# First stage of a spectral-filter kernel: half a column table mirrored on VectorE, angle arithmetic on GpSimd, statistics of two tiles on VectorE, 64-row products in fours

## Chip, cores and metric

The kernel runs on one core of one Trainium2 chip. The metric is the device time of one execution in microseconds (us). Five engines work side by side, each through its own instructions in program order: TensorE (PE; its weight loads are PEld), VectorE (DVE), ScalarE (ACT), GpSimd (POOL) and SyncE (SP), whose queue issues the transfers here. [...]

## What is computed

```
def _A_ref(x, w_r, w_i):
    X = rfft2(x.astype(float32), axes=(-2, -1))
    X = X * (w_r + 1j * w_i)
    return irfft2(X, s=(S, D)).astype(bfloat16)

def _B_ref(x, w_gate, w_up, w_down):
    return (gelu(x @ w_gate) * (x @ w_up)) @ w_down

h  = x + _A_ref(layernorm(x), A_w_r, A_w_i)
h2 = h + _B_ref(layernorm(h), B_w_gate, B_w_up, B_w_down)
```

S = 2048 rows, D = 576 columns, a hidden width of 4608, all data in bfloat16. `layernorm` subtracts the mean of a row and divides by its standard deviation.

## The kernel before

Everything is written as matrix products. The 2048 rows lie as 16 tiles of 128 partitions (row = 16 * partition + tile). The Fourier transform over rows is split in two: products with a 128-row table `F16` (called F in the profile) inside each tile, then products with twiddle tables. The transform over columns is a product with a cosine and sine table `DT` of 3 x 128 rows and 2 x 145 columns, and `DF`, two quarters of its third block. The stages, in order of time:

1. **First stage** (0 to about 25 us). Tables are made: POOL writes index ramps (`iota`), angles are reduced to a range that a sine can take, ACT takes the sines. Beside that each row tile is normalised. Its statistics come either from ACT (`ln_act`, L120 to 123: two passes, one for the sum and one for the squares, then POOL's `ln_fin`, L125 to 128) or from DVE (`ln_dve`, L114 to 118: two half-row passes and one that joins them). POOL makes the factor 1/standard deviation for four tiles at a time (`ln_rstd`, L130 to 133: an addition and a power). DVE writes the normalised tile `xn` (L136). PE multiplies it by `F16` (`row16`, L288 to 306: four products with 128 columns, L298, and two with the 64 leftover columns, `row16_rest`, L308). ACT copies the results out of PSUM into `Bt` (`evict`, L322; `evict4` for the leftover columns, L328).
2. **Column products and twiddles.** For one index after another, six products of `Bt` with `DT` and `DF` (`f2`, L479), a copy out of PSUM into `pq` (`f2_out`, L490), eight products with the twiddle table `TF` (`f3`, L496 and L497), a copy into `g` and `hs` (L518), sums and differences `xab` (L529), the multiplication with the weights (`wmul`, L547 to 568, all DVE), and the products of the inverse transform (`i3`, L587).
3. The inverse over columns (L638), the sum over rows (L770), the second normalisation.
4. The feed-forward part (L898 to L960), from 68 us to the end.

The order of the work is written by hand: a manual schedule is in force, so each engine runs its instructions in the order in which the Python calls stand. Lines 355 to 451 are that order for the first stage. `norms(lo, hi)` normalises tiles and issues their row products, `sd` asks for DVE statistics, `angle_a`, `angle_b`, `angle_c` reduce the angles of the twiddle table, `sine` and `cosine` (L253, L256) fill `TF`, `col_sin` (L347) fills `DT`, `turn_tf` (L262) transposes `TF` by DMA into `TI`. The twiddle table is done in two parts: `first` (2 of 9 blocks, 256 columns) and `rest` (7 blocks, 896 columns). All of its angles are made on DVE, as whole numbers: a multiplication with addition (L236), a mask by 2047 (L246), a subtraction (L247) and the removal of the sign (L223). The angles of `DT` are made on POOL up to a multiple of D (`kd`, L198, L199) and finished on DVE (`phases`, L268, and `drop_sign`).

POOL also runs two indirect gathers of weight rows (L381), clears `DF` and the `Zt` tiles (L387, L400) and halves two weight columns (L413). SP's queue issues the input, the two copies of the gathered weights (L411), `turn_tf(first)`, 13 copies of `DT` into `DQ` (L421), `turn_tf(rest)`, and then the weights of the later stages.

PSUM is held as four slots of two banks (`two`, L66), used in turn by `f2t`, `f4`, `pt`, `pq_ps`, `gh_ps` and so on: a product that opens a slot waits until the copy of its last user is done. `fill` (L283) issues products that nobody reads, 14 before tile 0, 8 before tile 8, 5 before tile 12 and 3 before `pt`, in places where PE would be idle.

Of the kernel before, what the change touches and what calls it, by code (L numbers as in the profile page):

```python
# [29 lines left out]
NFT = F // P  # L30
NR = D // 64
NDT = 5
JW = 58
NW = JP // JW
FQ = 3
# [6 lines left out]
def kernel_body(  # L42
# [140 lines left out]
    iota(kv[:, 0:7], [[1, 7]], 1)  # L183
    iota(kv[:, 7:9], [[8, 2]])
    q16 = tmp("q16", [P, P], FP32)
    iota(q16[:], [[16, P]])
# [4 lines left out]
    iJ = tmp("iJ", [P, JP], FP32)  # L191
    iota(iJ[:], [[1, 2], [2, JH]])
    iDs = tmp("iDs", [P, 3], FP32)
    G.tensor_scalar(iDs[:], iD[:], 1.0 / D, None, op0=ALU.mult)
    pd, kd = tmp("pd", [P, 3, JP], FP32), tmp("kd", [P, 3, JP], FP32)
    C23 = 8388608.0
    for t in range(3):
        G.tensor_scalar(kd[:, t, :], iJ[:], iDs[:, t : t + 1], C23, op0=ALU.mult, op1=ALU.add)  # L198
# [13 lines left out]
    ia, s2a, s2p = tmp("ia", [P, 1]), tmp("s2a", [P, 1], FP32), tmp("s2p", [P, 1], FP32)  # L212
    V.tensor_scalar(ia[:], ip[:], 7, None, op0=ALU.bitwise_and)
    V.tensor_scalar(s2a[:], ia[:], 127.0 / 8.0, None, op0=ALU.mult)
    V.scalar_tensor_tensor(s2p[:], ip[:], 0.125, s2a[:], op0=ALU.mult, op1=ALU.add)
    ks = tmp("ks", [P, 9], FP32)
    V.tensor_scalar(ks[:], kv[:], s2p[:, 0:1], None, op0=ALU.mult)
    V.tensor_scalar(iu[:], iu[:], 7, None, op0=ALU.bitwise_and)
    mask = tmp("mask", [P, P], FP32)
    V.tensor_scalar(mask[:], iu[:].rearrange("p c l -> p (c l)"), 0.0, None, op0=ALU.is_equal)  # L220

    def drop_sign(dst, src):
        V.tensor_scalar(  # L223
# [5 lines left out]
            op1=ALU.logical_shift_right,  # L229
        )  # L230

    pr, ab = tmp("pr", [P, 9, P]), tmp("ab", [P, 9, P], FP32)

    def angle_a(sl):
        n = sl.stop - sl.start
        V.scalar_tensor_tensor(  # L236
            pr[:, sl],
            q16[:].unsqueeze(1).to_broadcast([P, n, P]),
            s2p[:, 0:1],
            ks[:, sl].unsqueeze(2).to_broadcast([P, n, P]),  # L240
            op0=ALU.mult,
            op1=ALU.add,
        )

    def angle_b(sl):
        V.tensor_scalar(pr[:, sl], pr[:, sl], 2047, None, op0=ALU.bitwise_and)  # L246
        V.tensor_scalar(ab[:, sl], pr[:, sl], -1024.0, None, op0=ALU.add)  # L247

    def angle_c(sl):
        drop_sign(ab[:, sl], ab[:, sl])  # L250

    def sine(sl):
        A.activation(TF[:, sl, 2, :], pr[:, sl], ACT.Sin, bias=pib[:], scale=-2.0 * PI / S)  # L253

    def cosine(sl):
        A.activation(TF[:, sl, 1, :], ab[:, sl], ACT.Sin, bias=nhpib[:], scale=2.0 * PI / S)  # L256

    def minus_sine(sl):
        V.tensor_scalar(TF[:, sl, 0, :], TF[:, sl, 2, :], -1.0, None, op0=ALU.mult)
# [5 lines left out]

    def phases():
        for t in range(3):
            V.scalar_tensor_tensor(  # L268
                pd[:, t, :], iJ[:], iD[:, t : t + 1], kd[:, t, :], op0=ALU.mult, op1=ALU.add
            )  # L270

    def row_table():
        V.tensor_tensor(
            F16[:, 0:2, :],
            fs[:].unsqueeze(1).to_broadcast([P, 2, P]),
            mask[:].unsqueeze(1).to_broadcast([P, 2, P]),
            ALU.mult,
        )
        V.tensor_scalar(F16[:, 2, :], F16[:, 0, :], -1.0, None, op0=ALU.mult)

    ps_f = {}

    def fill(dst, n):  # L283

# [3 lines left out]
    def row16(h):  # L288
        if h % 2 == 0 or h == H - 1:
            ps_f[h] = two("f2t")  # L290
        if h % 4 == 0:
            ps_f["f4", h] = two("f4")
        f2t, b = (ps_f[h], 0) if h in ps_f else (ps_f[h - 1], 1)
        fill(f2t[:, b, :], {0: 14, 8: 8, 12: 5}.get(h, 0))
# [10 lines left out]
        if h < 12:  # L305
            row16_rest(h)

    def row16_rest(h):  # L308
        o = (h % 4) * P
# [17 lines left out]
    def evict4(h):  # L327
# [2 lines left out]
            ps_f["f4", h][:, 0].rearrange("p (h c l) -> p h c l", h=4, c=16),  # L330
        )

    def sd(*hs):
        for h in hs:
            ln_dve(mv, h)

    def norms(lo, hi):
        for h in range(lo, hi):
# [1 line left out]
            row16(h)  # L340

    wm = [tmp(n, [P, 8 * J], BF16) for n in ("wm_r", "wm_i")]
    xn_pool = tc.tile_pool(name="xn", bufs=1, side="right")
    xn = xn_pool.__enter__().tile([P, H, D], BF16, name="xn")

    def col_sin(r, src, bias):
        A.activation(  # L347
            DT[:, :, :, r, :],
            src[:].rearrange("p t (a j) -> p t a j", a=2),
            ACT.Sin,  # L350
            bias=bias[:],
            scale=-2.0 * PI / D,
        )

    first, rest = slice(0, 2), slice(2, 9)
    ln_act(1)
    ln_act(3)
    sd(0)
    row_table()
    sd(2)  # L360
    ln_fin(slice(1, 4, 2))
    ln_rstd(rstd, mv, 0, 4)
    sd(4, 6)
    norms(0, 4)
    ln_act(5)
    ln_act(7)
    ln_fin(slice(5, 8, 2))
    ln_rstd(rstd, mv, 4, 8)
    ln_act(9)
    evict(0)  # L370
    ln_act(11)
    evict4(0)
    evict(2)
    angle_a(first)
    angle_b(first)
    angle_c(first)
    sine(first)
    cosine(first)
    norms(4, 8)
    for t, w in zip(wm, (A_w_r, A_w_i)):  # L380
        G.indirect_dma_start(  # L381
            out=t[:],
            out_offset=None,
            in_=w.rearrange("(a r) j -> a (r j)", r=8),
            in_offset=bass.IndirectOffsetOnAxis(ap=rev[:, 0:1], axis=0),
        )
    G.memset(DF[:], 0.0)  # L387
    ln_fin(slice(9, 12, 2))
    sd(8, 10)
    ln_rstd(rstd, mv, 8, 12)  # L390
    evict(4, 6)
    evict4(4)
    ln_act(13)
    sd(12, 14)
    norms(8, 12)
    sd(15)
    ln_fin(slice(13, 14))
    ln_rstd(rstd, mv, 12, 16)
    for z in Zts:
        G.memset(z[:].rearrange("p a w b j -> p (a w b) j")[:, :, JW:], 0.0)  # L400
    phases()
    drop_sign(kd[:], pd[:])
    evict(8, 10)
    evict4(8)
    col_sin(1, pd, zerob)
    col_sin(0, kd, hpib)
    norms(12, 16)
    minus_sine(first)

    for w, t in ((WR, wm[0]), (WI, wm[1])):  # L410
        nc.sync.dma_start(w[:, 9 : H + 1, 0:J], t[:].rearrange("p (r j) -> p r j", r=8))  # L411
    for w in (WR, WI):
        G.tensor_scalar(w[:, :, 0 : J : J - 1], w[:, :, 0 : J : J - 1], 0.5, None, op0=ALU.mult)  # L413
    turn_tf(first)
    for r in (1, 0):
        for w in range(1 - r, NW):
            j0, j1 = w * JW, (w + 1) * JW
# [7 lines left out]
    for h in range(12, 16):  # L425
        row16_rest(h)
    evict(12, 14, 15)
    angle_a(rest)
    V.tensor_copy(DF[0:32], D3[0:32])
    V.tensor_copy(DF[96:128], D3[96:128])  # L430
    evict4(12)
    angle_b(rest)
    pt = two("pt")
    fill(pt[:, 1, :], 3)
    for x in range(2):
        for p0 in (0, 64):
# [4 lines left out]
                start=True,  # L441
                stop=True,
            )
    for sign in range(2):
        A.activation(
            G16[:, sign, :, :].rearrange("p x q -> p (x q)"),
            pt[:, 0, 0 : 2 * P],
            ACT.Copy,
            scale=G_SCALE if sign == 0 else -G_SCALE,
        )  # L450
    sine(rest)

    xn_pool.__exit__(None, None, None)
    spw = tc.tile_pool(name="spw", bufs=1)
# [565 lines left out]
```

## Time and profile before

| | us |
|---|---|
| median of 3 runs | 497.54 (497.31 to 497.56) |
| the profiled execution's own time | 497.44 |
| its span, first to last instruction | 495.66 |
| PE busy in the span | 487.6 |
| DVE, ACT, POOL busy in the span | 224.9, 161.6, 29.3 |
| first row product (L298) starts | 9.12 |
| first column product (L479) starts | 25.16 |
| first copy of `g` (L518) starts | 28.20 |
| first `xab` (L529) starts | 28.89 |
| first inverse product (L587) starts | 34.28 |
| feed-forward part starts | 68.36 |

Times of single instructions are microseconds from the start of the span. The profile gives for each engine its busy time, the busy share in 40 slices, the chain of work that ended last, and, as a timeline, each instruction with its start, its duration, its line and its operands.

### The profile page before, as it was taken

Reading aid. Unit: us, or ns where it says so; the run is one execution under the profiler, and the core shown is the slowest. Engines: PE = TensorE matmul, PEld = TensorE weight load, DVE = VectorE, ACT = ScalarE, POOL = GpSimd, SP = SyncE. Lnnn points to the kernel's source line nnn. Section 1 sums busy time; section 2 is a strip of 40 time slices with the busy share of each in tenths; the row PEclk is TensorE's granted clock in tenths of the full one; section 3 lists DMA queues with packets and bytes.
Section 4 is the critical chain, followed back from the end, with each engine's and each line's share of the span. In section 5 each row is a group of like instructions: output and inputs, shape, how many; then the busy total and the mean of one; then the engine's idle time right before and its main releaser. Section 6 shows DMA issues by size and latency. Waiting matters only on the chain.

```text
span 495.7 us, 12763 instructions
## 1 busy us (share of the span) xinstructions
PE 487.6 (98%) x5714; PEld 337.6 (68%) x5716; DVE 224.9 (45%) x443; ACT 161.6 (33%) x289; POOL 29.3 (6%) x78
## 2 busy tenths in 40 slices
PE   6999999999999999999999999999999999999997
PEld 3478789885579965555599855555799655555995
DVE  8999884698632157433311244333221333333111
ACT  8999873322211022323300123223110233232000
POOL 8500010011110001000000000000000000000000
PEclk9999999999999999999999999999999999999999
DMA  8739779969990039988730079977700288870000
GB/s 291 214 52 201 207 148 207 185 107 211 213 210 4 3 84 180 209 166 153 145 73 3 1 177 187 199 153 147 144 3 1 79 156 158 156 149 2 13 15 24
DMA packets 89549, 62.33 MB, mean 126 GB/s; under 512 B 23190, under 2 KB 88086, under 8 KB 89494
## 3 DMA queue, kind: packets, MB, share of 16 engines
q1 hardware_dynamic: 89206, 60.34, 61.5%
q0 software_dynamic: 288, 1.18, 0.8%
q8 instruction: 44, 0.72, 0.7%
q14 instruction: 11, 0.09, 0.1%
HBM read 52.65 MB, written 2.36 MB: 111 GB/s over the span
## 4 chain that ended last, share of the span: by engine, by line
PE 95%; POOL 2%; DVE 1%; ACT 1%; issue 0%; POOLq 0%
PE gu L898 57%; PE acc L941 27%; PE pq_ps L479 2%; PE cs_ps L638 2%; PE acc L960 2%; PE eo_ps L587 2%; PE y_ps L770 1%; PE gh_ps L497 1%; PE gh_ps L496 1%; DVE xn L136 1%; POOL rstd L133 0%; PE f2t L298 0%; ACT DT L347 0%; ACT Bt L322 0%; POOL kd L198 0%
## 5 line engine op out<-in xcount | busy, mean ns | idle before, releaser
L898 PE MATMUL gu<-Bt,wgu 64*128 64x512 bf16 (+1 forms) x2646 | 270.6, 363 | 0.0
L898 PEld LDWEIGHTS <-wgu 64*128 64x128 bf16 x2646 | 151.8, 94 | 115.3 <-issue 0.3
L907 DVE TENSOR_TENSOR P_sb<-g_sb,gu 128x512 bf16<-128x512 f32 (+1 forms) x156 | 100.4, 645 | 140.3 <-ACT g_sb L906 140.3
L906 ACT ACTIVATE g_sb<-gu 128x512 f32<-128x512 f32 (+1 forms) x156 | 88.0, 564 | 193.5 <-PE gu L898 193.5
L941 PEld LDWEIGHTS <-P_sb 64*128 64x128 bf16 x2160 | 122.2, 94 | 10.9
L941 PE MATMUL acc<-wd,P_sb 64*128 64x288 bf16 x1440 | 90.9, 283 | 0.0
L950 DVE TENSOR_TENSOR part<-part,acc 128x576 f32<-128x576 f32 x15 | 11.3, 755 | 112.6 <-ACT part L949 112.6
L949 ACT COPY part<-acc 128x576 f32<-128x576 f32 x15 | 9.6, 640 | 122.8 <-PE acc L941 122.8
L941 PE MATMUL acc<-wd_a,P_sb 64*128 64x288 bf16 x720 | 46.8, 283 | 0.0
L898 PE MATMUL gu<-Bt,wgu_e 64*128 64x256 bf16 (+1 forms) x162 | 12.5, 305 | 0.0
L795 DVE TENSOR_SCALAR hrow<-h_sb,mv,rstd 128x1152 bf16<-128x1152 bf16 x14 | 12.2, 868 | 0.6 <-POOL rstd L833 0.6
L479 PE MATMUL pq_ps<-DT,Bt 128*128 128x290 bf16 x64 | 12.3, 286 | 0.0
L286 PE MATMUL f2t<-h_sb,ident 128*128 128x512 bf16 x26 | 8.3, 473 | 3.9 <-DMA h_sb<-in_A_x_dram 3.9
L133 POOL TENSOR_TENSOR rstd<-rstd,mhalf 128x1 f32<-128x1 f32 (+1 forms) x16 | 11.7, 729 | 1.3
L952 DVE TENSOR_TENSOR h_sb<-h_sb,part 128x576 bf16<-128x576 bf16 x15 | 11.4, 758 | 0.5
L898 PEld LDWEIGHTS <-wgu_e 64*128 64x128 bf16 x162 | 10.4, 94 | 1.1
L479 PEld LDWEIGHTS <-Bt 128*128 128x128 bf16 x96 | 9.2, 97 | 2.5
L132 POOL TENSOR_SCALAR rstd<-mv 128x1 f32<-128x1 f32 (+1 forms) x16 | 4.0, 247 | 116.4 <-DVE mv L118 116.1
L638 PE MATMUL cs_ps<-DQ,EO 58*128 58x290 bf16 x144 | 10.8, 283 | 0.0
L490 ACT CAST pq<-pq_ps 128x580 bf16<-128x580 f32 x15 | 9.9, 663 | 0.2
L298 PE MATMUL f2t<-F,xn 128*128 128x256 bf16 x64 | 9.3, 275 | 0.6 <-DVE xn L136 0.6
L123 ACT ACTIVATE junk<-h_sb 128x576 bf16<-128x576 bf16 x14 | 9.4, 674 | 0.6 <-DMA h_sb<-in_A_x_dram 0.6
(138 smaller groups left out, 280.0 us busy)
## 6 DMA issues: line engine op xcount, KB each, us to landing
wgu<-in_B_w_gate_dram SPq DMA_DIRECT2D x46, 432.0 KB
wgu<-in_B_w_up_dram SPq DMA_DIRECT2D x46, 432.0 KB
wd_a<-in_B_w_down_dram SPq DMA_DIRECT2D x1, 1728.0 KB
wd<-in_B_w_down_dram SPq DMA_DIRECT2D x1, 1728.0 KB
wd<-in_B_w_down_dram SPq DMA_DIRECT2D x6, 288.0 KB
out_dram<-h_sb SPq DMA_DIRECT2D x3, 576.0 KB
h_sb<-in_A_x_dram SPq DMA_DIRECT2D x4, 288.0 KB
h_sb<-in_A_x_dram SPq DMA_DIRECT2D x2, 576.0 KB
```

The costliest lines, as they stand in the source:

```text
L133: G.tensor_tensor(dst[:, sl], dst[:, sl], mhalf[:, sl], ALU.pow)
L479: T.matmul(ps[:, par, 0:JP], lhsT=Bt[:, t, col], rhs=DT[:, t // 2, par] if t < 4 else DF[:, par], start=(t == par), stop=(t == 4),)
L587: T.matmul(pv[:, n], lhsT=z[:, a, w].rearrange("p b j -> p (b j)"), rhs=TI[:, ts[k], 1 - a : 3 - a, :], start=(a == 0), stop=(a == 1),)
L638: T.matmul(ps[:, e, 0:JP], lhsT=EO[x][rows, w, 2 * g : 2 * g + 2].rearrange("p h e k l -> p (h e k l)"), rhs=DQ[rows, w] if w or e else DT ...
L795: V.tensor_scalar(hrow[:], h_sb[:, h, :].rearrange("p (r k) -> p r k", k=64).unsqueeze(2).to_broadcast([P, NR, 2, 64]), mv2[:, h, 0:1], rs ...
L898: T.matmul(gu[:, c, 0:n], lhsT=w[rows, r, i * P : (i + 1) * P], rhs=hl[tcnk % 2][rows, r, lo:hi], start=(r == 0), stop=(r == NR - 1),)
L906: A.activation(g_sb, gu[:, 0, 0:n], ACT.Gelu_apprx_tanh)
L907: V.tensor_tensor(p_sb(f)[:, lo:hi], g_sb, gu[:, 1, 0:n], ALU.mult)
L941: T.matmul(accs[i][:, c, 0:DH], lhsT=p_sb(f)[rows, st * P : (st + 1) * P], rhs=wd[f // NWA][rows, f % NWA, c * DH : (c + 1) * DH], start=( ...
L950: V.tensor_tensor(part, part, accs[1][:, :, 0:DH], ALU.add)
L952: V.tensor_tensor(hv, hv, part, ALU.add)
L960: T.matmul(acc[:, 0, 0:DH], lhsT=p_sb(f)[:, st * P : (st + 1) * P], rhs=wd[f // NWA][:, f % NWA, cc], start=(f == 0), stop=(f == NFT - 1),)
```

## The change

Seven things change, all in the first stage and at its seam with the second.

- **Column table.** `DT` has 145 columns per half; a sine is now taken for 73 of them only (`JM = 73`), and DVE writes the other 72 by copying them in reverse with a sign per partition (`mirror`, four instructions). The ramps and angles for it shrink from 290 to 146 columns.
- **Angles on POOL.** `phases` and a new `wrap` (a sum of two 438-column tensors) move from DVE to POOL. All angles of the twiddle table become fp32 arithmetic on POOL: `angle_a` adds two tensors, `angle_b` scales and rounds (two instructions with constants) and adds two tensors. DVE keeps the removal of the sign, now taken from the signed angle. The sine of `rest` moves from before the first column products to after them.
- **Statistics.** Tiles 7 and 13 move from ACT to DVE. `sd` now issues the joining instruction of a tile between the two half-row passes of the next.
- **Leftover products.** The 64-column products of four tiles are issued together after the fourth (`rests`), in one slot opened there.
- **Order.** All statistics of tiles 8 to 15 stand ahead of the normalisation of tile 8; the first part of the angles stands on POOL ahead of the factor for tiles 12 to 15; the rest of the angles stands on POOL behind it, ahead of the clearing of `Zt` and the halving of the weight columns. The mirror, the minus of the first sine and the two copies into `DF` stand on DVE directly behind the normalisation of tiles 12 to 15.
- **Fills.** 13 before tile 0 and 10 before tile 8 in place of 14, 8 and 5.
- **Small ones.** The row table is masked and written in one instruction; the negative half of `G16` is made by DVE from the positive half.

```diff
-    V.tensor_scalar(ks[:], kv[:], s2p[:, 0:1], None, op0=ALU.mult)
+    V.tensor_scalar(ks[:], kv[:], s2p[:, 0:1], 0.125, op0=ALU.mult, op1=ALU.mult)
...
     def angle_a(sl):
         n = sl.stop - sl.start
-        V.scalar_tensor_tensor(
+        G.tensor_tensor(
             pr[:, sl],
             q16[:].unsqueeze(1).to_broadcast([P, n, P]),
-            s2p[:, 0:1],
             ks[:, sl].unsqueeze(2).to_broadcast([P, n, P]),
-            op0=ALU.mult,
-            op1=ALU.add,
+            ALU.add,
         )
     def angle_b(sl):
-        V.tensor_scalar(pr[:, sl], pr[:, sl], 2047, None, op0=ALU.bitwise_and)
-        V.tensor_scalar(ab[:, sl], pr[:, sl], -1024.0, None, op0=ALU.add)
+        G.tensor_scalar(ab[:, sl], pr[:, sl], 1.0 / S, C23, op0=ALU.mult, op1=ALU.add)
+        G.tensor_scalar(ab[:, sl], ab[:, sl], -C23, -float(S), op0=ALU.add, op1=ALU.mult)
+        G.tensor_tensor(pr[:, sl], pr[:, sl], ab[:, sl], ALU.add)
     def angle_c(sl):
-        drop_sign(ab[:, sl], ab[:, sl])
+        drop_sign(ab[:, sl], pr[:, sl])
...
     def phases():
         for t in range(3):
-            V.scalar_tensor_tensor(
-                pd[:, t, :], iJ[:], iD[:, t : t + 1], kd[:, t, :], op0=ALU.mult, op1=ALU.add
-            )
+            G.tensor_scalar(pd[:, t, :], iJ[:], iD[:, t : t + 1], None, op0=ALU.mult)
+    def wrap():
+        G.tensor_tensor(pd[:], pd[:], kd[:], ALU.add)
...
+    def rests(h):
+        ps_f["f4", h] = two("f4")
+        for i in range(4):
+            row16_rest(h + i)
...
     def sd(*hs):
         for h in hs:
-            ln_dve(mv, h)
+            st = roll.tile([P, 2, 6], FP32, name="st", tag="st", bufs=3)
+            V.bn_stats(st[:, 0, :], h_sb[:, h, 0:DH])
+            flush()
+            V.bn_stats(st[:, 1, :], h_sb[:, h, DH:D])
+            agg.append((h, st))
...
     def col_sin(r, src, bias):
         A.activation(
-            DT[:, :, :, r, :],
+            DT[:, :, :, r, 0:JM],
...
+    def mirror(r):
+        for a in range(2):
+            V.tensor_scalar(
+                DT[:, :, a, r, JM - a : JH - a], DT[:, :, a, r, JM - 2 :: -1], sgn[:, r : r + 1], None, op0=ALU.mult
+            )
```

`flush` joins the statistics that are still open. The order after the change, from the statistics on:

```
    for h in (1, 3, 5, 9, 11):
        ln_act(h)
    phases()
    row_table()
    sd(0, 2)
    minus_row()
    sd(4)
    ln_fin(slice(1, 4, 2))
    ln_rstd(rstd, mv, 0, 4)
    sd(6, 7)
    flush()
    norms(0, 4)
    rests(0)
    ln_fin(slice(5, 6))
    ln_rstd(rstd, mv, 4, 8)
    wrap()
    gather(0)
    gather(1)
    evict(0, 2)
    evict4(0)
    norms(4, 8)
    rests(4)
    sd(8)
    drop_sign(kd[:], pd[:])
    sd(10, 12)
    ln_fin(slice(9, 12, 2))
    ln_rstd(rstd, mv, 8, 12)
    evict(4)
    col_sin(1, pd, zerob)
    col_sin(0, kd, hpib)
    sd(13, 14, 15)
    flush()
    G.tensor_scalar(q16[:], q16[:], s2p[:, 0:1], None, op0=ALU.mult)
    angle_a(first)
    angle_b(first)
    ln_rstd(rstd, mv, 12, 16)
    G.memset(DF[:], 0.0)
    G.memset(DT[:, :, 1, :, JH - 1], 0.0)
    norms(8, 12)
    rests(8)
    angle_c(first)
    evict(6)
    evict4(4)
    sine(first)
    cosine(first)
    norms(12, 16)
    rests(12)
    evict(8, 10)
    evict4(8)
    mirror(1)
    mirror(0)
    minus_sine(first)
    V.tensor_copy(DF[0:32], D3[0:32])
    V.tensor_copy(DF[96:128], D3[96:128])
    angle_a(rest)
    angle_b(rest)
    evict(12, 14, 15)
    evict4(12)
```

Behind it follow, as before, the clearing of `Zt`, the copies of the gathered weights, `turn_tf(first)`, the halving of the weight columns and the 13 copies into `DQ`. After the first two `f2` of the second stage:

```diff
         if i == 0:
             f2(order[0] + 8)
-            angle_c(rest)
-            cosine(rest)
             for r in range(2):
                 f2_out(order[0] + 8, V.tensor_copy, slice(r, r + 1))
+            angle_c(rest)
+            sine(rest)
+            cosine(rest)
             minus_sine(rest)
+            V.tensor_scalar(G16v[1], G16v[0], -1.0, None, op0=ALU.mult)
```

More of the change, by code (lines that the diff above doesn't have):

```diff
@@ L32 @@
 NDT = 5
+JM = 73
 JW = 58
@@ L185, in kernel_body @@
     q16 = tmp("q16", [P, P], FP32)
-    iota(q16[:], [[16, P]])
+    iota(q16[:], [[2, P]])
     make_identity(nc, ident[:])
@@ L211, in kernel_body @@
     )
[L212 to L215, printed above, removed]
+    V.tensor_scalar(iu[:], iu[:], 7, None, op0=ALU.bitwise_and)
+    odd, sgn = tmp("odd", [P, 1]), tmp("sgn", [P, 2], FP32)
+    s2p = tmp("s2p", [P, 1], FP32)
+    V.tensor_scalar(odd[:], ip[:], 1, None, op0=ALU.bitwise_and)
+    V.scalar_tensor_tensor(s2p[:], iu[:, 0, 0:1], 127.0, ip[:], op0=ALU.mult, op1=ALU.add)
+    for r, s in ((0, -2.0), (1, 2.0)):
+        V.tensor_scalar(sgn[:, r : r + 1], odd[:], s, -0.5 * s, op0=ALU.mult, op1=ALU.add)
     ks = tmp("ks", [P, 9], FP32)
[L217 to L220 removed]
+    V.tensor_scalar(ks[:], kv[:], s2p[:, 0:1], 0.125, op0=ALU.mult, op1=ALU.mult)
     def drop_sign(dst, src):
@@ L331, in evict4, with flush @@
         )
+    agg = []
+    def flush():
+        while agg:
+            h, st = agg.pop()
+            V.bn_aggr(mv[:, h, :], st[:])
     def sd(*hs):
         for h in hs:
-            ln_dve(mv, h)
+            st = roll.tile([P, 2, 6], FP32, name="st", tag="st", bufs=3)
[3 more added lines that the diff above has]
+            agg.append((h, st))
     def norms(lo, hi):
@@ L342, in kernel_body, with gather @@
     wm = [tmp(n, [P, 8 * J], BF16) for n in ("wm_r", "wm_i")]
+    def gather(i):
+        G.indirect_dma_start(
+            out=wm[i][:],
+            out_offset=None,
+            in_=(A_w_r, A_w_i)[i].rearrange("(a r) j -> a (r j)", r=8),
+            in_offset=bass.IndirectOffsetOnAxis(ap=rev[:, 0:1], axis=0),
+        )
     xn_pool = tc.tile_pool(name="xn", bufs=1, side="right")
@@ L364, in kernel_body @@
+    flush()
     norms(0, 4)
-    ln_act(5)
-    ln_act(7)
-    ln_fin(slice(5, 8, 2))
+    rests(0)
+    ln_fin(slice(5, 6))
     ln_rstd(rstd, mv, 4, 8)
-    ln_act(9)
-    evict(0)
-    ln_act(11)
+    wrap()
+    gather(0)
+    gather(1)
+    evict(0, 2)
     evict4(0)
-    evict(2)
+    norms(4, 8)
+    rests(4)
+    sd(8)
+    drop_sign(kd[:], pd[:])
+    sd(10, 12)
+    ln_fin(slice(9, 12, 2))
+    ln_rstd(rstd, mv, 8, 12)
+    evict(4)
+    col_sin(1, pd, zerob)
+    col_sin(0, kd, hpib)
@@ L374, in kernel_body @@
+    sd(13, 14, 15)
+    flush()
+    G.tensor_scalar(q16[:], q16[:], s2p[:, 0:1], None, op0=ALU.mult)
     angle_a(first)
     angle_b(first)
+    ln_rstd(rstd, mv, 12, 16)
+    G.memset(DF[:], 0.0)
+    G.memset(DT[:, :, 1, :, JH - 1], 0.0)
+    norms(8, 12)
+    rests(8)
     angle_c(first)
+    evict(6)
+    evict4(4)
     sine(first)
     cosine(first)
[L379 to L398, printed above, removed]
+    norms(12, 16)
+    rests(12)
+    evict(8, 10)
+    evict4(8)
+    mirror(1)
+    mirror(0)
+    minus_sine(first)
+    V.tensor_copy(DF[0:32], D3[0:32])
+    V.tensor_copy(DF[96:128], D3[96:128])
+    angle_a(rest)
+    angle_b(rest)
+    evict(12, 14, 15)
@@ L399, in kernel_body @@
+    evict4(12)
     for z in Zts:
         G.memset(z[:].rearrange("p a w b j -> p (a w b) j")[:, :, JW:], 0.0)
[L401 to L408, printed above, removed]
     for w, t in ((WR, wm[0]), (WI, wm[1])):
         nc.sync.dma_start(w[:, 9 : H + 1, 0:J], t[:].rearrange("p (r j) -> p r j", r=8))
+    turn_tf(first)
     for w in (WR, WI):
         G.tensor_scalar(w[:, :, 0 : J : J - 1], w[:, :, 0 : J : J - 1], 0.5, None, op0=ALU.mult)
-    turn_tf(first)
@@ L423, in kernel_body @@
                     )
[L425 to L432, printed above, removed]
     pt = two("pt")
@@ L443, in kernel_body @@
             )
[L444 to L451, printed above, removed]
+    G16v = [G16[:, sign].rearrange("p x q -> p (x q)") for sign in range(2)]
+    A.activation(G16v[0], pt[:, 0, 0 : 2 * P], ACT.Copy, scale=G_SCALE)
     xn_pool.__exit__(None, None, None)
```

35 lines of the change are left out of this document (16 added, 19 removed).

## Prediction

> **What bounds the kernel now.** I read the busy shares in 40 slices first, to see which stage has idle time, then the chain of work that ended last, then the timeline of each engine from 0 to 38 us.
>
> ```profile
> PE   6999999999999999999999999999999999999997
> DVE  8999884698632157433311244333221333333111
> ACT  8999873322211022323300123223110233232000
> POOL 8500010011110001000000000000000000000000
> ```
>
> PE is full from the second slice to the end (487.6 of 495.7 us), so time can only be won or lost where the first stage hands over to PE. POOL is nearly free after 25 us, which is the room that the change uses. The chain of work across the seam:
>
> ```profile
> 19.90 1.01 ACT Bt L322
> ...
> 21.28 1.95 ACT DT L347 x2
> 23.23 0.91 ACT Bt L322
> ...
> 25.22 2.34 PE pq_ps L479 x18
> ```
>
> In the tail of the first stage ACT ends last: a copy, 1.95 us of column sines, three more copies to 25.10, and then the column products (first one at 25.16 in the timeline). From there PE has no gap until 34.03. What follows hangs on the copy of `g`, behind the twiddle sines on ACT, and on DVE:
>
> ```profile
> 25.80 1.04 ACT L253 ACTIVATE TF<-pr,pib 128x896 bf16<-128x896 int32 x1
> 26.74 0.64 ACT L490 CAST pq<-pq_ps 128x580 bf16<-128x580 f32 x1
> 27.26 1.06 ACT L256 ACTIVATE TF<-ab,nhpib 128x896 bf16<-128x896 f32 x1
> 28.20 0.65 ACT L518 CAST g<-gh_ps 128x578 bf16<-128x578 f32 x1
> ```
>
> ```profile
> 28.89 1.43 DVE L529 TENSOR_TENSOR xab<-g,gh_ps 128x578 bf16<-128x578 bf16 x2 [0.74 <-ACT g L518]
> ...
> 34.09 0.76 DVE L547 TENSOR_TENSOR m<-xab,WR 128x1156 bf16<-128x1156 bf16 x1
> ...
> 37.66 0.76 DVE L547 TENSOR_TENSOR m<-xab,WR 128x1156 bf16<-128x1156 bf16 x1
> ```
>
> `xab` starts when `g` is copied, and from 28.89 DVE runs without a gap, one index per 3.57 us (34.09 to 37.66); PE's inverse products wait about 0.2 us for it each time. So whatever moves the start of the `g` copy (28.20) moves the rest of the program by as much. That start is the yardstick of all sums below.
>
> **Without mutual holds.** ACT loses two tiles of statistics (2 x 2 passes of 0.67, L123: 2.7 us), 0.75 of column sines (438 elements in place of 870; between the 256-element sine of 0.51 and the 870-element one of 1.04 the slope is 0.86 ns, so 0.66 each) and one G copy (0.28). It is no longer last.
>
> DVE loses the angles (L236 0.48 and 1.14, L246, L247, L223, `phases` 1.33), and gains two tiles, four mirrors and a G copy. A tile cost 0.925 (13.88 to 14.80); with the join slid between other passes it is about 0.82. Normalising tile 4 can start at 11.0 instead of 11.54, as its factor no longer waits for ACT's tile 7. Then 4 x 0.34, six tiles at 0.82, half of L223 (0.31) and a last join: tile 8 at about 17.5, 0.9 later than now (16.66), since tiles 13 and 15 now stand ahead of it.
>
> POOL, in its order: factor 4 to 7 done at 10.9, `wrap`, two gathers at about 1.0 (13.9), the factor for 8 to 11, which needs tile 10 (16.0), then `q16` 0.41, the first angles and the factor for 12 to 15 (two instructions, 1.5). One input with constants costs 0.24 at 4 elements (L132) and 0.93 at 870 (L199): 0.79 ns an element. A sum of two long tensors on POOL stands nowhere in the trace: the rows are L127 and L128, 2 elements, 0.19. It can't be cheaper than one input (0.79 ns), and I take as its upper end both operands read one after the other (1.58 ns): 256, 438 and 896 elements are 0.39 to 0.59, 0.54 to 0.88, 0.90 to 1.61. I take the upper ends, since two operands are streamed. The first angles are then 2.6 us, the factor stands at 20.4 (now 20.96), and tile 12 is normalised then (now 21.00). Four tiles 1.36, four mirrors at 0.19 (L259, 0.22 for 256 bf16), minus 0.14, two `DF` copies 0.6, the leftover copy 0.7: the first column product at 24.0, 1.1 earlier.
>
> That gain is given back before the yardstick. Now the sine of `rest` runs ahead of the `pq` copy and `g` follows the first product by 3.04 us. After the change DVE has the two copies of the second product first (it ends 1.65 after the first product starts; 0.74), then the sign (0.63), then ACT the cosine (1.06): `g` follows by about 4.0. 24.0 + 4.0 = 28.0 against 28.20. This would be no change.
>
> **The hold.** Now the rows that decide. POOL and DVE hold each other when both work on SBUF:
>
> ```profile
> 4.41 1.19 POOL L198 TENSOR_SCALAR kd<-iJ,iDs 128x290 f32<-128x290 f32 x2
> ```
>
> ```profile
> 4.84 0.37 DVE L273 TENSOR_TENSOR F<-fs,mask 128x256 bf16<-128x256 f32 x1
> 5.25 0.40 DVE L279 TENSOR_SCALAR F<-F 128x128 bf16<-128x128 bf16 x1
> ```
>
> ```profile
> 23.64 0.29 DVE L429 COPY DF<-DT 32x580 bf16<-32x580 bf16 x1
> 23.94 0.43 DVE L430 COPY DF<-DT 32x580 bf16<-32x580 bf16 x1
> ```
>
> ```profile
> 23.77 0.40 POOL L413 TENSOR_SCALAR WI<-WI 128x34 bf16<-128x34 bf16 x1 [1.80 <-DVE pr L236]
> ```
>
> L279 takes 0.40 for 128 elements where L259 takes 0.22 for 256; the POOL pair beside it ends at 5.60, and L279 at 5.64. The two `DF` copies are alike, but the one that meets the halving of WI takes 0.43 instead of 0.29, and ends 0.2 behind it. POOL is held too: its 2-element L128 at 9.41 takes 0.38 instead of 0.19 while tiles are normalised, and yet it gets in between two of them. So they alternate, each waiting for the whole instruction of the other. Now the POOL instructions are short where DVE needs SBUF. After the change they are long, right there.
>
> Step by step at the upper prices: `wrap` (10.9 to 11.8) holds tile 4 by 0.6, and tile 8 is normalised at 18.3. Tiles 8 to 11 and the first angles hold each other, and the factor is ready at 21.4 (+1.0). The clearing of `DF` (0.60, L387) holds tile 12, which ends at 22.2. Then the four instructions of `rest` come one by one (1.6, 1.1, 1.1, 1.7 with their own waits of 0.1), and one DVE instruction passes between each two: tile 13 ends at 23.9, tile 14 at 25.0, tile 15 at 26.1. No row shows a copy that reads in reverse; held by nothing, the mirrors end at 26.9, and held as the copies are, behind the last POOL instruction, at 28.3. I take the first. The minus, `DF` and the leftover copy, partly held, end at 29.0. First column product 29.05, `g` at 33.1: **+4.9 us**. Held mirrors make it +6.0. With sums at 0.79 ns the whole is 2.1 to 2.3 less: +2.8.
>
> [...]
>
> **What costs nothing.** Four fills fewer and the leftover products in fours lie in PE's waits for tiles 4 and 8 (with fills or without, PE waits there). SP's order is unchanged; its 13 `DQ` copies (24.14 to 34.00) start as late as the first minus, but are read first at 50.83, and `turn_tf(rest)` lands at 39.8 for a product at 41.5, which shifts too. The halving of the weights on POOL moves behind `rest` and ends near 29; its first reader, the multiplication with the weights (L547), comes only after `xab`, past 34.
>
> **The rivals.**
> - *DVE keeps its turn.* If back-to-back DVE instructions don't let POOL in, DVE runs through from 21.4 to 24.2, and the four instructions of `rest` start then: 5.3 us to 29.5, sine and cosine 2.0, `g` at 31.5: +3.3, 500.7. Against it speaks L128 getting in at 9.41.
> - *No hold of long instructions.* All holds shown are 0.1 to 0.2 us long. If a long POOL instruction leaves DVE room, the sum without holds stands: `g` at 28.0 to 28.3, 497.4.
> - *Faster.* As before, and POOL's first angles take at most 1.2 us instead of 2.6. Then tile 12 is normalised right behind tile 11 at 19.2, the first column product comes at 22.9 and `g` at 26.9: −1.3, 496.1. It decides from where the factor for 12 to 15 is ready by 19.2; the 0.24 that even 4 elements cost on POOL speaks against it.
>
> **How the numbers follow.** The profiled execution took 497.44, its span 495.66 with 1.78 around it; the median of the runs is 497.54, 0.10 more. Forecast 497.44 + 4.9 = 502.3, chance 0.58, with its own range 500.0 to 505.0. DVE keeps its turn 0.18, no hold 0.15, faster 0.09. A measurement of this kernel can tell 0.2% (1.0 us) from no change. Slower 0.58 + 0.18 = 0.76, same 0.15, faster 0.09. The range is 497.0 to 505.0: it takes in the case without holds and both prices, and leaves out the faster one and the tail above +7.6 (0.08).
>
> **What would show it.** The first column product near 29, `g` near 33, tiles 13 to 15 taking over 0.9 each in place of 0.42 and ending just behind a POOL instruction, and the feed-forward part starting 4 to 6 us later than 68.36. [...] Tiles 13 to 15 at 0.42 beside a long POOL instruction would make the forecast wrong; a tile 12 before 19.5 would make the faster rival right.

## Result and profile after

The changed kernel takes 505.09 us (median of 6 runs, 504.98 to 506.86); the kernel before, on the same chip, 497.55 (497.31 to 498.30). The ratio is 1.016, 95% interval 1.0144 to 1.0177. The forecast was 502.3, its range ended at 505.0. The direction and the place were right, and so was the mutual hold of POOL and DVE, but the forecast left the mirrors out of it; the size was too small by 2.8 us.

The profiled execution took 505.04, its span 503.3. The busy shares in 40 slices:

```profile
PE   5679999999999999999999999999999999999997
DVE  6879976489651127633312145333212233333111
...
POOL 8840000011110001100000000000000000000000
```

PE's row is new in its first three digits only (6, 9, 9 before), and POOL is now busy through its second slice (8, before 5) and into its third (4, before 0). The whole loss lies ahead of the third slice's end. The chain of work that ended last, from the fourth group of tiles on:

```profile
21.74 1.05 POOL rstd L134
22.79 0.03 issue
22.81 4.47 DVE xn L137 x4
27.29 2.92 DVE DT L387 x4
...
30.31 0.35 DVE DF L444
...
31.02 0.70 DVE Bt L335
...
31.76 1.66 PE pq_ps L507 x12
...
34.97 1.04 ACT TF L256
36.01 0.53 ACT g L546
```

Before, ACT ended last here; now POOL and then DVE do. Four tiles take 4.47 us and four mirrors 2.92. The yardstick, the start of the first `g` copy, is 35.91 in the timeline in place of 28.20: 7.7 later, and the span is 7.6 longer. Behind it nothing is lost or won: the feed-forward part starts at 75.96 in the chain of work in place of 68.36, again 7.6 later. The next two fences are DVE's and POOL's timelines of the changed kernel (start, duration, line): tiles 13 to 15 and the first mirror, and the four instructions of the rest of the angles.

```profile
23.46 1.78 DVE L137 TENSOR_SCALAR xn<-h_sb,mv,rstd 128x576 bf16<-128x576 bf16 x1
25.16 1.10 DVE L137 TENSOR_SCALAR xn<-h_sb,mv,rstd 128x576 bf16<-128x576 bf16 x1
26.18 1.10 DVE L137 TENSOR_SCALAR xn<-h_sb,mv,rstd 128x576 bf16<-128x576 bf16 x1
27.21 2.54 DVE L387 TENSOR_SCALAR DT<-DT,sgn 128x216 bf16<-128x216 bf16 x1
```

```profile
23.32 1.76 POOL L237 TENSOR_TENSOR pr<-q,ks 128x896 f32<-128x896 f32 x1
25.16 0.94 POOL L245 TENSOR_SCALAR ab<-pr 128x896 f32<-128x896 f32 x1
26.18 0.94 POOL L246 TENSOR_SCALAR ab<-ab 128x896 f32<-128x896 f32 x1
27.21 2.08 POOL L247 TENSOR_TENSOR pr<-pr,ab 128x896 f32<-128x896 f32 x1
```

Read them as pairs. Each DVE instruction ends 0.16 to 0.17 behind its POOL partner (23.46 + 1.78 = 25.24 against 25.08), the mirror 0.46 behind (short POOL clears follow there). A tile that takes 0.42 alone took as long as whatever POOL did beside it: 1.78, 1.10 and 1.10 beside 1.76, 0.94 and 0.94. That is the alternation of the forecast.

### The profile page after: what moved, and what is told of

Its sections match the earlier page's. It is cut to its first block, busy times and chain, and to the rows that moved or that the text cites. A ratio compares the mean times of both kernels' runs of the same rounds, so it can differ in the third digit from the quotient of the medians.

```text
span 503.3 us, 12756 instructions
## 1 busy us (share of the span) xinstructions
PE 487.6 (97%) x5712; PEld 339.1 (67%) x5712; DVE 227.8 (45%) x445; ACT 158.7 (32%) x280; POOL 39.0 (8%) x90
## 4 chain that ended last, share of the span: by engine, by line
PE 92%; POOL 3%; DVE 3%; ACT 1%; issue 0%; POOLq 0%
PE gu L928 56%; PE acc L971 26%; PE cs_ps L666 2%; PE pq_ps L507 2%; PE acc L990 2%; PE eo_ps L615 2%; DVE xn L137 1%; PE y_ps L800 1%; POOL rstd L134 1%; PE gh_ps L525 1%; PE gh_ps L524 1%; DVE DT L387 1%; POOL pd L268 0%; PE eo_ps L639 0%; PE pt L869 0%
## 5 line engine op out<-in xcount | busy, mean ns | idle before, releaser
L971 PEld LDWEIGHTS <-P_sb 64*128 64x128 bf16 x2160 | 122.2, 94 | 10.9
L302 PEld LDWEIGHTS <-xn 128*128 128x128 bf16 x64 | 6.1, 106 | 10.4 <-DVE xn L137 9.1
L137 DVE TENSOR_SCALAR xn<-h_sb,mv,rstd 128x576 bf16<-128x576 bf16 x16 | 10.3, 703 | 3.4 <-POOL rstd L134 3.4
L292 PE MATMUL f2t<-h_sb,ident 128*128 128x512 bf16 x23 | 6.8, 456 | 3.7 <-DMA h_sb<-in_A_x_dram 3.7
```

The costliest lines, as they stand in the source:

```text
L137: eng.tensor_scalar(dst, h_sb[:, h, :], m[:, h, 0:1], r[:, h : h + 1], op0=ALU.subtract, op1=ALU.mult)
L302: T.matmul(f2t[:, b, t * 2 * P : (t + 1) * 2 * P], lhsT=x[:, d0 : d0 + P], rhs=F16[:, n : n + 2, :], start=(n == 0), stop=(n == 1),)
L971: T.matmul(accs[i][:, c, 0:DH], lhsT=p_sb(f)[rows, st * P : (st + 1) * P], rhs=wd[f // NWA][rows, f % NWA, c * DH : (c + 1) * DH], start=( ...
```

## Experiments

**Is it POOL, and what about it?** Five kernels are the kernel before with sums on POOL that nothing reads, behind the factor for tiles 12 to 15.

```diff
     ln_rstd(rstd, mv, 12, 16)
+    for i in range(3):
+        G.tensor_tensor(
+            dm[0:128],
+            dm[0:128] if i else q16[0:128].unsqueeze(1).to_broadcast([128, 7, P]),
+            ks[0:128, 2:9].unsqueeze(2).to_broadcast([128, 7, P]),
+            ALU.add,
+        )
```

*Three long sums.* Expected:

> The kernel before, with three sums of 128x896 fp32 added on POOL behind the factor for tiles 12 to 15; nothing reads their result, each reads the one before it. Hold theory (a DVE instruction with one source in SBUF waits for the whole POOL instruction, and one passes between two): POOL runs them from 21.0 to 26.9 (1.76 to 2.08 each), tiles 12, 13 and 14 end just behind one each (22.9, 24.9, 27.0), tile 15 takes 0.42; minus, angles of rest, two DF copies and the leftover copy follow, first column product 30.1 in place of 25.16, time +5.0, 502.5. Rival (POOL off the path costs nothing to DVE, and the slow tiles of the changed kernel have another cause): tiles at 0.42, 497.5.

Measured 503.23 (502.97 to 503.68), ratio 1.0112 (1.0095 to 1.0129): +5.7. The second sum in POOL's timeline and tile 13 in DVE's:

```profile
22.77 1.68 POOL L401 TENSOR_TENSOR dm<-dm,ks 128x896 f32<-128x896 f32 x1
```

```profile
22.78 1.84 DVE L136 TENSOR_SCALAR xn<-h_sb,mv,rstd 128x576 bf16<-128x576 bf16 x1
```

The tiles end at 22.86, 24.62, 26.78 and 27.11 where 22.9, 24.9, 27.0 and 27.4 were expected. POOL work that nobody waits for cost DVE its own length here: tiles of 1.79 and 1.84 beside sums of 1.68, where a tile alone takes 0.42. The leftover copy ends at 30.03 as forecast, but the first column product starts at 30.97: PE, which had waited for the tiles, had a granted clock (the share of its full clock, as the profile shows it) of 0.50 to 0.54 from 26 to 32, so some 0.9 us of the profiled execution's loss is the clock's, estimated from the 30.1 expected for that start.

*The same sums on 32 partitions.*

```diff
-            dm[0:128],
+            dm[0:32],
```

The inputs are cut in the same way. Expected:

> The same three sums on 32 of the 128 partitions: the same number of elements for each partition, a quarter of the bytes. Hold of whole instructions: as with 128 partitions, tiles 12 to 14 end at 22.9, 24.9 and 27.0, time +5.0, 502.5. Rival (the engines share the bytes that SBUF can move): a quarter of the tiles' extra time at most, time +0.5 to +1.2, 498.0 to 498.7.

Measured 503.04 (502.53 to 503.24), +5.5; sums of 1.67, tiles of 1.79 and 1.83. A quarter of the bytes changed nothing (+5.7 with all of them), so it is not a sharing of all the bytes that move. A sharing inside each partition would look the same here; the next experiment leaves the work of each partition as it was.

*The same sums in short pieces.*

```diff
+    for i in range(3):
+        for k in range(7):
+            G.tensor_tensor(
+                dm[:, k], dm[:, k] if i else q16[:], ks[:, 2 + k : 3 + k].to_broadcast([P, P]), ALU.add
+            )
```

Expected:

> The same sums of 128 partitions cut into 21 instructions of 128 elements each, as much work in all. Hold of whole instructions: a DVE instruction waits for one piece of about 0.3 at most, tiles 12 to 15 take about 0.7 each, tile 15 ends at 23.9, and the minus, the angles and the DF copies wait about 0.25 each: time +1.5 to +2.5, 499.0 to 500.0. Rival (shared bytes): the same work, so the same as the three long sums, +5.0. If POOL's pieces come without a gap for DVE, worse than that: +6 or more.

Measured 498.93 (498.92 to 499.01), +1.4. Tile 13 in DVE's timeline:

```profile
21.49 0.50 DVE L136 TENSOR_SCALAR xn<-h_sb,mv,rstd 128x576 bf16<-128x576 bf16 x1
```

The same work in 21 pieces costs a quarter, and not all of that is holds: `g` starts 1.0 late (29.16), and later the multiplication with the weights waits 0.71 for POOL's halving, which stands behind the pieces. Tiles and pieces still alternate one to one, a pair every 0.42 to 0.43, though a tile alone takes 0.34 from start to start and a piece 0.39: by these lengths only a part of each instruction kept the other out. So the cost went with the length of the single POOL instruction (+5.7 with three sums of 1.68), and a sharing inside the partitions falls too.

*Tiles in the form with two sources.*

```diff
+                V.scalar_tensor_tensor(
+                    xn[:, h, :],
+                    h_sb[:, h, :],
+                    mv[:, h, 0:1],
+                    rstd[:, h : h + 1].to_broadcast([P, D]),
+                    op0=ALU.subtract,
+                    op1=ALU.mult,
+                )
```

This form is used for tiles 12 to 15, beside the three long sums. Expected:

> The three long sums again, and tiles 12 to 15 normalised by the form of DVE instruction with two tensor sources (the factor, repeated along the row, is the second). If only DVE instructions with one source in SBUF are held: these tiles take 0.65 to 0.7 each beside the sums and tile 15 ends at 23.6; the minus (one source) waits until 24.9, the DF copies until 26.9, first column product 28.2, time +3.1, 500.6. If every DVE instruction that uses SBUF is held: tiles 12 to 14 end behind one sum each, and four tiles cost 0.25 more each, time +6, 503.5.

Measured 504.28 (504.15 to 504.48), +6.7: held too.

```profile
21.06 2.24 DVE L342 SCALAR_TENSOR_TENSOR xn<-h_sb,mv,rstd 128x576 bf16<-128x576 bf16 x1 [0.28 <-POOL rstd L133]
...
27.54 0.80 DVE L342 SCALAR_TENSOR_TENSOR xn<-h_sb,mv,rstd 128x576 bf16<-128x576 bf16 x1
```

These are tiles 12 and 15. Tile 15, beside short POOL work, takes 0.80; tile 12 ends 0.61 behind the sum that ends at 22.69. Here POOL waits as well: its second and third sums take 2.08 in place of 1.68.

*Two sums that needn't wait for each other.*

```diff
+    for d in range(2):
+        G.tensor_tensor(
+            dms[d][:],
+            q16[:].unsqueeze(1).to_broadcast([P, 7, P]),
+            ks[:, 2:9].unsqueeze(2).to_broadcast([P, 7, P]),
+            ALU.add,
+        )
```

Expected:

> The kernel before, with two sums of 128x896 fp32 added on POOL behind the factor for tiles 12 to 15, into different tiles, so that the second needn't wait for the first (in the three long sums each waited about 0.08 for the one before it). If DVE gets one instruction between two POOL instructions in any case: tile 12 ends 0.17 behind the first sum (22.9), tile 13 behind the second, time +2.8 to +3.2, 500.5. If DVE gets its turn only where POOL's next instruction has to wait: tile 12 stays held through both sums and the three short clears behind them, to about 24.9, tiles 13 to 15 follow at 0.34 each, time about +3.4, 501.0; the end of tile 12 tells the two apart.

Measured 500.95 (499.96 to 502.51), +3.5. The times spread too far to tell the two apart (the profiled execution is the one of 499.96, the only one with a granted clock of 1.00 over its whole span), but the trace does: tile 12 ends at 22.53, 0.17 behind the first sum (22.36), so DVE got its turn without a wait on POOL's side.

What is *not* held shows in the changed kernel itself, in the timelines of POOL and of DVE near 18.6:

```profile
18.65 0.61 POOL L237 TENSOR_TENSOR pr<-q,ks 128x256 f32<-128x256 f32 x1
```

```profile
18.70 0.40 DVE L354 BATCH_NORM_STATS2 st<-h_sb 128x6 f32<-128x288 bf16 x1
```

A statistics pass takes 0.40 beside a sum of 0.61, as it does alone, and the pass at 5.92 of the kernel before takes 0.43 beside a POOL instruction of 870 elements and 0.93 (L199 there, at 5.68); the leftover copy out of PSUM takes 0.69 beside POOL's pieces and without them. No run here has a statistics pass beside an 896-element sum.

**Are the mirrors dear by themselves?** First the changed kernel with POOL's rest of the angles released by the copies into `DF`, through one POOL instruction that depends on them:

```diff
+    G.tensor_scalar(D3[0:1, 0, 0, 0:1], D3[0:1, 0, 0, 0:1], 1.0, None, op0=ALU.mult)
     angle_a(rest)
```

Expected:

> The changed kernel, with POOL's four instructions of the rest of the angles released only by the end of DVE's copies into DF (a POOL instruction that needs them stands ahead). Hold theory: nothing of POOL lies beside tiles 13 to 15 and the mirrors; these take 0.42 and 0.2 to 0.3 each, the first column product comes at 27.0 in place of 31.76. POOL makes the rest from 26.3 to 32.1, its sign and cosine follow, g at about 34.1 in place of 35.91: time -1.8, 503.3. Rival (the mirror is slow by itself, as it reads in reverse, and the tiles are slow for another reason): mirrors 3.0 as before, first column product at 31 or later, and the rest later still: 507 or more.

DVE's timeline, tiles 13 to 15 and the mirrors:

```profile
23.45 1.09 DVE L137 TENSOR_SCALAR xn<-h_sb,mv,rstd 128x576 bf16<-128x576 bf16 x3
24.47 0.87 DVE L387 TENSOR_SCALAR DT<-DT,sgn 128x216 bf16<-128x216 bf16 x4
```

Tiles 0.42 each, mirrors 0.28 for 216 elements, where the minus takes 0.21 for 256: reading in reverse cost little here. The first column product starts at 26.85 and `g` at 33.95, both about as expected. The time was still 504.94 (503.06 to 505.53). PE had waited 3.65 us for `g`, and its granted clock was 0.81 from 35 to 36 and then 0.50 (the windows of PE: window, length, PE busy, granted clock):

```profile
36.00:39.00 3.00, 3.00 (x14) 0.50 0.40 81
```

Most of the gain was lost there. The one run with a mean granted clock of 0.999 took 503.06, near the 503.3 expected; the other three (0.990 to 0.997) took 504.50 to 505.53.

Then the changed kernel without mirrors. It leaves out half of the column table, which stays a constant:

```diff
     D3 = DT[:, 2]
+    V.memset(DT[:], 0.5)
...
-    mirror(1)
-    mirror(0)
```

Expected:

> The changed kernel without its four mirrors; the other half of the column table is set to a constant early, so this part of the computation is left out. The mirrors' group shows 3.0 busy. Rival (that is their price): the end comes 3.0 earlier, g at 32.9, 502.1. Hold theory: the place of the first mirror behind tile 15 (27.29) is taken by the minus of the first sine, which then waits for POOL's last sum until 29.3; only the mirrors' own 0.8 is saved: first column product at 30.9, g at 35.1, 504.3.

Measured 504.68 (504.56 to 504.95). The minus slips in ahead of POOL's last sum, and the first copy into `DF` takes the mirror's place: 2.59, from 27.71 to 30.30. The time is 0.4 below that of the changed kernel. Setting the constant delays tile 8 by 0.4 (19.64 against 19.26); even with that added back a group of 3.0 busy was worth 0.8. Most of its time was a wait, and the next in line inherits it.

**Which part carries the loss?** The rest of the angles back on DVE as whole numbers (`angle_v`, the three DVE instructions of the kernel before), behind the leftover copy:

```diff
-    angle_a(rest)
-    angle_b(rest)
     evict(12, 14, 15)
     evict4(12)
+    angle_v(rest)
```

Expected:

> The changed kernel, with the rest of the angles made on DVE again as whole numbers (1.14, 0.63, 0.63), behind the leftover copy; all else as changed. Hold theory: tile 12 at 22.8, tiles 13 to 15 and the mirrors at their own lengths, held only by the short POOL instructions that move up (0.4), first column product at 27.2; the angles end at 29.7, the two copies of the second product and the sign follow, cosine, g at 32.0: time -3.9, 501.2. Rival (POOL is the cheaper place for them, as it was free): DVE loses 2.4 more and the time is not below that of the changed kernel, 505 or more.

Measured 501.05 (501.02 to 501.12), ratio to before 1.0071 (1.0056 to 1.0087). First column product 27.21, `g` 31.92. And with the first part back as well, and POOL's clears of `Zt` and halvings released by the copies into `DF`:

```diff
     flush()
+    angle_v(first)
+    drop_sign(ab[:, first], ab[:, first])
     norms(0, 4)
...
-    G.tensor_scalar(q16[:], q16[:], s2p[:, 0:1], None, op0=ALU.mult)
-    angle_a(first)
-    angle_b(first)
     ln_rstd(rstd, mv, 12, 16)
...
+    G.tensor_scalar(D3[0:1, 0, 0, 0:1], D3[0:1, 0, 0, 0:1], 1.0, None, op0=ALU.mult)
     evict(12, 14, 15)
```

Expected:

> The changed kernel with all angles of the twiddle table made on DVE again as whole numbers (the first part in DVE's wait for the first factor, the rest behind the leftover copy), and POOL's clears of Zt and halvings released only by the copies into DF. Mirrors, wrap, statistics and leftover products as changed. Hold theory: the factor for tiles 12 to 15 at 20.9, tile 12 then, tiles and mirrors at their own lengths, first column product at 24.7 (before: 25.16); the rest of the angles stands between that and the copies of the second product, so g at 29.3, +1.1: 498.7. Rival (the change's other parts cost as well): no better than with only the rest on DVE, 501.

Measured 499.08 (498.77 to 499.19), 1.0032 (1.0019 to 1.0045). So of +7.5 the rest on POOL carries 4.0. The second step gives 2.0: tile 12 comes 1.5 earlier (21.22 in place of 22.72), and the four tiles take 1.74 in place of 2.20, as POOL's clears no longer lie beside them, so the first part alone carries about 1.5. What remains, 1.6, is above all the order at the seam: the first column product comes at 25.46 (before 25.16), but `g` follows by 4.6 in place of 3.0, with the angles, the sign and the cosine of the rest in between.

**Fills and products by fours alone**, in the kernel before:

```diff
-        fill(f2t[:, b, :], {0: 14, 8: 8, 12: 5}.get(h, 0))
+        fill(f2t[:, b, :], {0: 13, 8: 10}.get(h, 0))
...
     norms(0, 4)
+    rests(0)
```

Expected:

> The kernel before with the leftover products issued by fours and the changed number of fills (13 and 10 in place of 14, 8 and 5), nothing else. The prediction's claim: they lie in PE's waits, 497.3 to 497.8. Rival: without the fills ahead of tile 12, or with the leftover products behind the tiles, PE's clock falls or the leftover copy comes later, 498.5 or more.

Measured 498.45, but in two groups: four runs at 497.19 to 497.52, seven at 498.43 to 498.79. The windows of PE (window, length, PE busy, granted clock) from 20 on, of the kernel before and of the profiled one of these, which took 498.79:

```profile
20.00:22.00 2.00, 1.66 (x11) 1.00 0.96 284
22.00:24.00 2.00, 1.82 (x22) 1.00 0.07 20
```

```profile
20.00:22.00 2.00, 0.29 (x3) 1.00 0.90 265
22.00:24.00 2.00, 2.00 (x14) 0.67 0.06 17
24.00:26.00 2.00, 2.00 (x13) 0.50 0.54 107
```

With no fills ahead of tile 12 PE is nearly idle from 20 to 22 (it waits 2.46 for tile 12), and then its clock is 0.67 and 0.50: the leftover copy waits 0.54 for PE, and the first column product starts at 26.46. With the old fills:

```diff
-        fill(f2t[:, b, :], {0: 13, 8: 10}.get(h, 0))
+        fill(f2t[:, b, :], {0: 14, 8: 8, 12: 5}.get(h, 0))
```

Expected:

> The kernel before with the leftover products by fours, but with the old fills (14, 8 and 5). With the changed fills this part alone gave 497.2 to 497.5 in four runs and 498.4 to 498.8 in seven, and in the profiled one PE's granted clock was 0.67 and 0.50 from 22 to 26, with no fills ahead of tile 12. If the missing fills are the cause: clock 1.0, all runs at 497.2 to 497.5. If the products by fours are (their PE wait at tile 12, or the later leftover copy): again runs at 498.5.

Measured 497.32 (497.17 to 497.72), ratio 1.000 (0.999 to 1.0009), clock 1.00 throughout. The fills were the cause, by the windows the five ahead of tile 12 (those ahead of tiles 0 and 8 went back as well); the products by fours are free. And the changed kernel with fills:

```diff
-    FILL = {0: 13, 8: 10}
+    FILL = {0: 13, 8: 10, 12: 5, 13: 3, 14: 3, 15: 3}
```

Expected:

> The changed kernel with 5 fills ahead of tile 12 and 3 ahead of each of tiles 13, 14 and 15, in PE's waits of about 1 us; they write where the tile's products write next. The changed kernel's clock was 0.81 from 26 to 28 and 0.50 from 28 to 30. If DVE behind POOL sets the end there, the clock may rise to 1.0 and the time stays at 505.0 to 505.1. If the low clock has a share of the +7.5: first column product earlier by up to 0.5, 504.5.

Measured 504.52 (504.45 to 504.72). At a granted clock of 1.00 PE is through with its products into `pt` at 29.4 and takes the first four column products from 29.99, ahead of the leftover copy; `g` starts at 35.37. The low clock had 0.5 to 0.6 us of the loss. Why the changed kernel, with PE through at 30.7, doesn't start these four ahead of the copy's end as well is not shown.

**A version without the holds?** POOL's two long sums go ahead of the factor for 8 to 11, to run beside statistics passes; rounding of the rest is on ACT; the first angles are on DVE, ahead of tile 0; the last sum of the rest is on DVE, behind the leftover copy; the cosine of the rest behind `g`.

```diff
-    wrap()
     gather(0)
     gather(1)
+    wrap()
+    angle_a(rest)
...
+    A.activation(ab[:, rest], pr[:, rest], ACT.Identity, bias=c23[:], scale=1.0 / S)
+    A.activation(ab[:, rest], ab[:, rest], ACT.Identity, bias=c23s[:], scale=-float(S))
...
     evict4(12)
+    V.tensor_tensor(pr[:, rest], pr[:, rest], ab[:, rest], ALU.add)
```

Expected:

> An attempt to keep what the change wins and avoid the holds. POOL's two long sums (column angles, first sum of the rest) run beside DVE's statistics passes, which showed no hold; rounding and scaling of the rest run on ACT while it waits; the first angles are whole numbers on DVE in its wait for the first factor, the clearing of DF too; the last sum of the rest (about 1.0) is DVE's, behind the leftover copy; other POOL work is released by the copies into DF; the cosine of the rest stands behind the first copy of g. Hold theory: tile 8 at 19.5, tile 12 at 20.9, four tiles 1.4, mirrors 0.8, first column product at 24.5, g at 27.4 in place of 28.20: time -0.8, 496.7. Rival (statistics passes are held as well, or what follows g takes the gain back): no better than before, 497.5 or more.

Measured 501.49 (501.23 to 503.00), slower than before. In DVE's timeline one tile takes 3.53:

```profile
14.00 3.53 DVE L139 TENSOR_SCALAR xn<-h_sb,mv,rstd 128x576 bf16<-128x576 bf16 x1
```

Tile 6 was not through when POOL's second gather (13.56 to 14.57) and the two sums behind it (14.59 to 17.35) came, and was held by all of them. So the long sums never ran beside statistics passes, and the placement that was meant stays untested. The attempt also started DVE 1.5 later (tile 0 at 11.34 against 9.82), as input landed later (ACT's last wait for it ends at 9.43 against 8.30) and the first angles stood ahead of it. No version here beats the kernel before.

## Why the prediction was wrong in size

| | forecast | measured |
|---|---|---|
| factor for tiles 4 to 7 | 10.9 | 11.82 |
| factor for tiles 8 to 11 | 16.0 | 17.95 |
| tile 8 normalised | 18.3 | 19.26 |
| tile 12 normalised | 21.4 | 22.81 |
| tile 15 ends | 26.1 | 27.29 |
| mirrors end | 26.9 (28.3 held) | 30.21 |
| leftover copy ends | 29.0 | 31.71 |
| first column product | 29.05 | 31.76 |
| `g` starts | 33.1 | 35.91 |

- **The hold, right.** Tiles 13 to 15 and POOL's instructions alternate, as the `DF` rows and L128 of before had said; the long sums, alone or on 32 partitions, show it by themselves (tiles of 1.84 and 1.83 beside sums of 1.68 and 1.67). Both rivals that doubted it fall: DVE did not keep its turn (tile 13 took 1.78), and long instructions held as short ones did (a tile took 1.84 beside a sum of 1.68, and 0.50 beside a piece of 0.39). "When both work on SBUF" was too wide, though: tiles with two sources were held (2.24 beside 1.68), but a statistics pass over `h_sb` was not (0.40 beside a sum of 0.61). The faster rival falls too: tile 12 came at 22.8, not before 19.5.
- **The step that failed: the mirrors, taken as "held by nothing".** The forecast named both ends, 26.9 and 28.3, and chose the lower for want of a row, though by its own rule of alternation POOL's last sum lay beside them; the held price stood in its range without a chance of its own. They ended at 30.2, so this step alone missed 2.1 (1.2 late at tile 15's end, 3.3 late at the mirrors'). Without POOL beside them they take 0.28 each; the 2.54 of the first is POOL's last sum, itself 0.4 longer than forecast (2.08 against 1.7).
- **The price of the sums, too low.** 896 elements cost 1.76 with repeated operands and 2.08 with two full ones, 256 cost 0.61 and 0.73, 438 cost 1.11; the forecast's upper ends were 1.61, 0.59 and 0.88. That a sum costs twice the one-input price (1.58 ns an element), with both operands read one after the other, was the author's estimate; the runs show the lengths, not how the operands are read. The rest took 5.97 in place of 5.5.
- **The start, too early.** `phases` on POOL stands in no sum of the forecast: three instructions of 0.65 to 0.68 for 146 elements each (5.93 to 7.88), ahead of the first factor, for which DVE then waits 1.60 (0.18 before). The timelines of POOL and of DVE:

```profile
5.93 1.95 POOL L268 TENSOR_SCALAR pd<-iJ,iD 128x146 f32<-128x146 f32 x3
```

```profile
9.82 1.45 DVE L137 TENSOR_SCALAR xn<-h_sb,mv,rstd 128x576 bf16<-128x576 bf16 x4 [1.60 <-POOL rstd L134]
```

Tile 0 is normalised at 9.82 (8.63 before) and tile 4 at 11.86 in place of 11.0. POOL falls back further, as `wrap` takes 1.11 and the gathers end at 15.60 in place of 13.9, but that is not what counts next: POOL waits 0.48 for DVE's statistics of tile 10, which stand behind the late and held tiles 4 to 7, before it can make the factor for 8 to 11. That factor is 1.9 late; POOL's way from there to the factor for 12 to 15 (4.83) is 0.6 shorter than forecast with holds. This is read from the trace; no run took it back alone.
- **The tail, too dear.** From the mirrors' end to the leftover copy's end 2.1 were forecast, 1.5 measured. From the first column product to `g` 4.05 and 4.15.
- **A claim that fell: "four fills fewer ... lie in PE's waits".** The products do; the fills kept PE's clock up, worth 1.2 us in most runs of that part alone and about 0.5 here.

Added up at `g`: +1.4 to tile 12, -0.2 over the tiles, +2.1 mirrors, -0.6 tail, +0.1: 2.8, which is the whole miss.

## To carry to other kernels

Before work moves to an idle POOL, list what DVE does in the same microseconds. Here a normalisation took 1.78 beside a POOL instruction of 1.76, a mirror (out of SBUF and into it) 2.54 beside one of 2.08, a normalisation in the form with two sources 2.24 beside one of 1.68. So long POOL instructions belong beside nothing of this kind, or beside what was not held here (statistics passes beside POOL instructions of up to 0.93, the leftover copy out of PSUM beside pieces of about 0.4), or must be cut short (+1.4 in 21 pieces, +5.7 in three sums). A group whose busy time is a wait is not a saving: take it out, and the next instruction waits in its place (2.59 for a copy where the first mirror had taken 2.54). Products that nobody reads may be what keeps PE's clock (0.67 and 0.50 without the five ahead of tile 12, 1.00 with them), so price their removal by the granted clock behind the gap.

## What the runs showed of the hardware beyond that

- The length of one wait doesn't settle PE's granted clock. It was 0.50 for about 3 us behind a wait of 3.65, and 0.67 and 0.50 behind one of 2.46 (the two groups of times say that this happened in seven runs of eleven). In the changed kernel it was 0.60 and 0.55 behind a wait of 2.03 ahead of tile 8, but 1.00 in the same place with the rest of the angles on DVE (the eight leftover products take 0.64 and 0.41, and that run's mean clock was 1.000); and in the changed kernel it was 0.50 from 28 to 30 behind waits of 1.00, 0.41 and 0.41 only. What does settle it is not shown.
- POOL instructions of one input differ more than their lengths do. `phases` (a factor per partition and nothing else) takes 0.65 for 146 elements; L199 of the changed kernel (`kd`, a factor per partition and a constant added) takes 0.39 for the same 146, and L246 (two constants) 0.41 for 256. So the factor per partition alone isn't the reason, and what is stays open.
- Why one tile stayed held by a gather and two sums in a row (3.53), while two sums in a row elsewhere let a tile through (22.53), stays open.
